# Premix on four quarters of TensorE's array, mix on its row halves, with five tokens to each piece

## The chip, the cores and the metric

The kernel runs on one core of a Trainium2 chip. The metric is the device time of one execution in microseconds (us). A core has a matrix engine (TensorE, PE in the profile, with its weight loads shown apart as PEld), a vector engine (VectorE, DVE), a scalar engine (ScalarE, ACT), a general engine (GpSimd, POOL) and a sync engine (SyncE, SP) that here issues nearly all DMAs. Sixteen DMA engines move data between the memory of the chip (HBM) and the core's on-chip memory (SBUF), and from one place of SBUF to another. Matmuls write to PSUM, an accumulator memory of its own.

## The reference

The kernel computes an attention that mixes its heads before and after the softmax, and behind it an MLP with `g = h - tanh(h)`:

```python
scale = 1.0 / np.sqrt(q.shape[-1])
scores = scale * np.matmul(q, k.transpose(0, 1, 3, 2))
scores = np.einsum('bhij,hg->bgij', scores, w_pre)
scores = scores - np.max(scores, axis=-1, keepdims=True)
attn = np.exp(scores)
attn = attn / (np.sum(attn, axis=-1, keepdims=True) + 1e-09)
attn = np.einsum('bhij,hg->bgij', attn, w_post)
attn_out = np.matmul(attn, v)
...
x = np.ascontiguousarray(attn_out.transpose(0, 2, 1, 3)).reshape(B * S, H * D)
h = x @ w_in
g = h - np.tanh(h)
return (g @ w_out).astype(np.float32)
```

q, k and v are (8, 12, 448, 64): B = 8 batches, H = 12 heads, S = 448 tokens, D = 64. `w_pre` and `w_post` are 12 x 12. x is 3584 x 768, `w_in` 768 x 2048, `w_out` 2048 x 768. All inputs and the output are float32.

## The kernel before

**Blocks, groups, places.** The 448 query tokens of a batch are cut in four blocks of 120, 120, 120 and 88, 32 blocks in all. The scores of a block lie in an SBUF tile `s` with tokens on partitions and [head, key] along each. To mix heads on TensorE, heads must lie on partitions, so a block is cut in groups of at most ten tokens, and a DMA, the gather (L493), brings a group from `s` into a tile `t` whose partitions are (token, head): 120 rows of 448 keys (108 for a group of nine). There are 360 groups. Two groups make one of 180 places, and a place is one turn of the loop that starts at L818. The MLP follows the loop.

**What a place does.** In written order, which every engine keeps: the copy out of PSUM of the mix before (`at`, L566 or L573); the gathers of groups 2p+4 and 2p+5; up to six other queued DMAs (`issue`, L370); `premix` of place p; `norm` of place p-1; `split` of group 2p+3; `expo` of place p; the jobs that the table `todo` has for the place; the scores' evictions from PSUM; `mix` of place p-1; and one step of the conversion of the MLP's weights (`conv`, helpers at L38 to L110, on ACT, DVE and GpSimd, with loads and stores of its own).

**Premix** (L508) multiplies a group with a block-diagonal matrix that holds `w_pre` ten times, `wpre` [120, 120]. The even group of a place takes one fp32 matmul (L512), which the hardware runs in two passes. The odd group is split beforehand: `th` is its value rounded to fp32r (L504, DVE), `tl` the rest (L505, GpSimd). It takes three fp32r matmuls of one pass each (L515 to L517), with `wpre` split likewise. The tiles `t` of even groups have three buffers, those of odd ones two.

**Expo, norm, mix.** `expo` takes the row maximum on DVE (L527) and the exponential on ACT (L529) with the row sum in `zs`. `norm` adds 1e-9 (L541), takes the reciprocal (L543), both on DVE, and makes one weight tile for each group on ACT: `wr = wpost / sum` (L545), with `wpost` the block-diagonal matrix of `w_post`. `mix` (L548) uses the exponentials `e` as weights of the array, 112 keys at a time, and moves `wr` through: eight fp32 matmuls of 120 columns (L557) into the one buffer of `ps_o`, which gives the mixed attention with keys on partitions.

**The jobs of `todo`.** Scores of two head pairs (L475): three fp32r matmuls for each head, the two heads of a pair on the two row halves of the array, since D = 64. Their evictions (L481) go to ACT and DVE for even pairs, both to ACT for odd ones. Values (L598): fp32 matmuls on the two column halves. Transposes of queries (L441) and keys (L415). Loads of queries, keys and values. A planner sets the places. The keys of a batch are loaded from one place before the place where block 1 of the batch before starts (L785), one of three tiles a place. Their transposes stand two places later or more (L791).

**DMA order.** SP issues its DMAs in written order, gathers and loads in one stream. A tile's buffers go round, so a gather can't be issued before the matmul (or the split) that read the tile's buffer last has ended.

The helper `halves` (L405) is `(slice(0, 64), slice(64, 128))`. NG = 360, NPL = 180, GI = 10, GP = 120.

Of the kernel before, what the change touches and what calls it, by code (L numbers as in the profile page):

```python
# [10 lines left out]
F32 = mybir.dt.float32  # L11
# [10 lines left out]
def raw(ap):  # L22

    return ap.bitcast(F32)
# [124 lines left out]
def kernel_body(  # L149
# [19 lines left out]
    GI = P // H  # L169
    MT = GI * H  # L170
    GP = GI * H
    starts = list(range(0, S, MT))
    sizes = [min(MT, S - s) for s in starts]
    NM = len(sizes)
# [162 lines left out]
    with ExitStack() as st:  # L337
# [127 lines left out]
        def scores(i, hp, engines=None):  # L465

            b, m = blocks[i]
            n = sizes[m]
            if hp == 0:
                sts[i] = sp.tile([MT, H, S], F32, name="s", tag="s")  # L470
            (qh, ql), (kh, kl) = qbs[i], kks[b, hp // 2]
            pss = [ps_m.tile([P, 512], F32, name="ps_q", tag="ps_m") for _ in halves]
            for x, (qx, kx) in enumerate(((qh, kh), (qh, kl), (ql, kh))):
                for a, ps in zip(halves, pss):
                    nc.tensor.matmul(ps[:n, :S], qx[a, hp, :], kx[a, hp % 2], start=(x == 0), stop=(x == 2))  # L475

            def rest():

                two = engines or (nc.scalar.copy, nc.scalar.copy if hp % 2 else nc.vector.tensor_copy)
                for j, (eng, ps) in enumerate(zip(two, pss)):  # L480
                    eng(sts[i][:n, 2 * hp + j, :], ps[:n, :S])  # L481

            sooner.append(rest)
# [7 lines left out]
        tg, ts, te = {}, {}, {}  # L491

        def gather(t, eng=nc.sync):  # L493
            i, g = groups[t]
            x = gp.tile([GP, S], F32, name="t", tag=f"t{t % 2}", bufs=3 - t % 2)
            eng.dma_start(x[: rows[t], :], sts[i][tokens[t].start : tokens[t].stop : tokens[t].step])
            tg[t] = x

        def split(t, eng=nc.gpsimd):
            n = rows[t]  # L500
            x = tg.pop(t)
            th = gp.tile([GP, S], F32R, name="th", tag="th", bufs=2)
            tl = gp.tile([GP, S], F32R, name="tl", tag="tl", bufs=2)
            nc.vector.tensor_copy(th[:n, :], x[:n, :])  # L504
            eng.tensor_sub(tl[:n, :], x[:n, :], raw(th[:n, :]))  # L505
            ts[t] = (th, tl)

        def premix(p):  # L508

            pa, pb = [ps_p.tile([P, S], F32, name="ps_p", tag="ps_p") for _ in range(2)]  # L510
            n = rows[2 * p]
            nc.tensor.matmul(pa[:n, :], wpre[:n, :n], tg.pop(2 * p)[:n, :], start=True, stop=True)  # L512
            n = rows[2 * p + 1]
            th, tl = ts.pop(2 * p + 1)
            nc.tensor.matmul(pb[:n, :], wph[:n, :n], th[:n, :], start=True, stop=False)  # L515
            nc.tensor.matmul(pb[:n, :], wpl[:n, :n], th[:n, :], start=False, stop=False)
            nc.tensor.matmul(pb[:n, :], wph[:n, :n], tl[:n, :], start=False, stop=True)  # L517
            return pa, pb

        def expo(p, pss):  # L520
            zs = gp.tile([GP, 3, 2], F32, name="zs", tag="zs")
            es = []
            for j, ps in enumerate(pss):
                n = rows[2 * p + j]

                mx = gp.tile([GP, 1], F32, name="mx", tag="mx")
                nc.vector.tensor_reduce(out=mx[:n, :], in_=ps[:n, :], axis=AX.X, op=ALU.max, negate=True)  # L527
                e = gp.tile([GP, S], F32, name="e", tag="e", bufs=4)
                nc.scalar.activation(  # L529
                    e[:n, :], ps[:n, :], AF.Exp, bias=mx[:n, :], scale=1.0, accum_out=zs[:n, 0, j : j + 1]  # L530
                )
                es.append(e)
            te[p] = [es, zs]

        def norm(p):
            zs = te[p][1]
            wr = gp.tile([GP, 2, P], F32, name="wr", tag="wr", bufs=2)[:, :, :GP]
            n0, n1 = rows[2 * p], rows[2 * p + 1]
            for j, n in enumerate((n0, n1)):

                nc.vector.tensor_scalar_add(zs[:n, 1, j : j + 1], zs[:n, 0, j : j + 1], 1e-9)  # L541
            for js, n in ((slice(0, 2), n0),) if n0 == n1 else ((slice(0, 1), n0), (slice(1, 2), n1)):
                nc.vector.reciprocal(zs[:n, 2, js], zs[:n, 1, js])  # L543
            for j, n in enumerate((n0, n1)):
                nc.scalar.mul(wr[:n, j, :], wpost[:n, :], zs[:n, 2, j : j + 1])  # L545
            te[p].append(wr)

        def mix(p):  # L548
            es, _, wr = te.pop(p)
            ps = ps_o.tile([P, 2, 512], F32, name="ps_o", tag="ps_o")  # L550
            for j, e in enumerate(es):
                i, g = groups[2 * p + j]
                n = rows[2 * p + j]
                if g == 0:
                    ats[i] = kp.tile([CP, NC, H, MT], F32, name="at", tag="at", bufs=2)
                for c in range(NC):
                    nc.tensor.matmul(  # L557
                        ps[:CP, j, c * GP : (c + 1) * GP], e[:n, c * CP : (c + 1) * CP], wr[:n, j, :],
                        start=True, stop=True,
                    )  # L560

            def rest():
                (i0, _), (i1, _) = groups[2 * p], groups[2 * p + 1]
# [84 lines left out]
        now()  # L648
        load_q(2)
        now()  # L650
        tmp_w = kp.tile([P, 2 * GP + 2 * H], F32, name="tmp_w", tag="at", bufs=2)
        w12 = tmp_w[:H, 2 * GP : 2 * GP + 2 * H].rearrange("p (w h) -> p w h", w=2)
        nc.scalar.dma_start(w12[:, 0, :], w_pre)
        nc.scalar.dma_start(w12[:, 1, :], w_post)

# [8 lines left out]
        def scores_of(i, hq):  # L664
# [7 lines left out]
        prep_q(0, 1)  # L672
        flush()

        repeat = tmp_w[:H, GP : 2 * GP]
        nc.gpsimd.memset(repeat, 0.0)
        nc.gpsimd.affine_select(
            out=repeat.rearrange("p (i h) -> p i h", i=GI), in_=repeat.rearrange("p (i h) -> p i h", i=GI),
            compare_op=ALU.not_equal, fill=1.0, base=0, pattern=[[0, GI], [-1, H]], channel_multiplier=1,
        )  # L680
        ps_w = bank()[:GP, : 2 * H].rearrange("p (w g) -> p w g", w=2)
        nc.tensor.matmul(ps_w.rearrange("p w g -> p (w g)"), repeat, w12.rearrange("p w g -> p (w g)"), start=True, stop=True)
        wpre, wpost = [cst.tile([GP, P], F32, name=x)[:, :GP] for x in ("wpre", "wpost")]
        pre_v = wpre.rearrange("p (i g) -> p i g", i=GI)
        post_v = wpost.rearrange("p (g i) -> p g i", i=GI)
        nc.vector.tensor_copy(pre_v, ps_w[:, 0, :].unsqueeze(1).to_broadcast([GP, GI, H]))
        nc.vector.tensor_copy(post_v, ps_w[:, 1, :].unsqueeze(2).to_broadcast([GP, H, GI]))
        for x, step in ((pre_v, [[H, GI], [0, H]]), (post_v, [[0, H], [H, GI]])):

            nc.gpsimd.affine_select(  # L690
                out=x, in_=x, compare_op=ALU.is_ge, fill=0.0, base=0, pattern=[[-a, n] for a, n in step],
                channel_multiplier=1,
            )
            nc.gpsimd.affine_select(
                out=x, in_=x, compare_op=ALU.is_ge, fill=0.0, base=H - 1, pattern=step, channel_multiplier=-1,
            )


        busy(3, ps_b)
# [17 lines left out]
        prep_q(1, 0)  # L717
        prep_q(1, 1)
        flush()
        wph, wpl = [cst.tile([GP, P], F32R, name=x)[:, :GP] for x in ("wph", "wpl")]  # L720
        nc.vector.tensor_copy(wph, wpre)
        nc.vector.tensor_sub(wpl, wpre, raw(wph))
# [6 lines left out]
        split(1, nc.vector)  # L729
# [88 lines left out]
        for p in range(NPL + 3):  # L818
# [117 lines left out]
```

## Time and profile before

| what | value |
| --- | --- |
| runs, median (all) | 1879.54 us (1880.68, 1879.54, 1875.44) |
| profiled execution | 1880.95 us |
| its span | 1879.2 us |
| its granted TensorE clock | 0.998 |
| ACT's exponentials L529, in 360 instructions | all on 120 or 108 partitions |
| HBM traffic over the span | 156 GB/s |

The span is the profiled time from the first to the last instruction. The page cuts it in 40 slices of 47 us and gives the busy share of each engine in tenths; the MLP begins in slice 20:

```profile
## 2 busy tenths in 40 slices
PE   8999999999999999999999999999999999999998
...
DVE  5676766767776676766456556556566566565555
ACT  5787887878888788788634443434434434433433
POOL 2344444444444345444201000000000000000000
...
DMA packets 232795, 371.92 MB, mean 198 GB/s; under 512 B 98992, under 2 KB 207536, under 8 KB 218288
```

A digit of 9 is 90% or more. In the loop (the left half) PE is busy throughout, ACT to 70 or 80%, DVE to 60 or 70%, GpSimd to 40%; DMA is the mean share of the sixteen DMA engines, so 6 can be all of them at 60% or ten of them at nearly all.

### The profile page before, as it was taken

The page shows a single profiled execution, that of the slowest core. Times are in us where ns is not written, and L with a number is a line of the kernel's source. Part 1 is how long each engine was busy: PE and PEld are TensorE (multiplying, and loading weights), DVE is VectorE, ACT ScalarE, POOL GpSimd, SP SyncE. Part 2 cuts the span into 40 slices and gives each one's busy share as a digit, 9 for nine tenths or more (in the row PEclk, how much of TensorE's full clock was granted, in tenths as well). Part 3 has the DMA queues.
Part 4 walks back from the last instruction along what each step waited for, and adds up shares of the span by engine and source line. Part 5 has one row for each costly group of instructions (what it writes and reads, how often), then busy time and mean ns, then how long its engine had stood idle before and what let it go on. Part 6 is the DMA issues. An engine that isn't in the chain of part 4 may idle for free.

```text
span 1879.2 us, 35344 instructions
## 1 busy us (share of the span) xinstructions
PE 1851.1 (99%) x13150; PEld 1525.9 (81%) x13150; DVE 1184.7 (63%) x2457; ACT 1133.8 (60%) x2503; POOL 451.9 (24%) x401
## 2 busy tenths in 40 slices
PE   8999999999999999999999999999999999999998
PEld 6777887787878777877788888888888888888887
DVE  5676766767776676766456556556566566565555
ACT  5787887878888788788634443434434434433433
POOL 2344444444444345444201000000000000000000
PEclk9999999999999999999999999999999999999999
DMA  6667658676675757656565565665655655655651
GB/s 162 183 183 201 189 166 221 182 208 190 177 216 171 209 177 205 195 164 189 212 255 193 206 246 192 223 218 196 235 213 196 235 205 196 237 209 191 233 193 42
DMA packets 232795, 371.92 MB, mean 198 GB/s; under 512 B 98992, under 2 KB 207536, under 8 KB 218288
## 3 DMA queue, kind: packets, MB, share of 16 engines
q1 hardware_dynamic: 231740, 368.45, 60.5%
q8 instruction: 104, 1.70, 0.4%
q10 hardware_dynamic: 884, 1.22, 0.2%
q14 instruction: 67, 0.55, 0.1%
HBM read 245.37 MB, written 47.19 MB: 156 GB/s over the span
## 4 chain that ended last, share of the span: by engine, by line
PE 86%; DMA 6%; ACT 3%; DVE 2%; issue 2%; POOL 1%; SPq 0%; ACTq 0%; POOLq 0%; DVEq 0%
PE ps_o L557 13%; PE ps_h L256 8%; PE ps_h L260 8%; PE ps_h L255 8%; PE ps_m L598 7%; PE ps_p L512 6%; PE ps_q L475 6%; PE ya L303 5%; PE ya L300 5%; PE ya L301 5%; DMA t<-s 4%; PE yb L303 3%; PE yb L301 3%; PE yb L300 3%; PE ps_p L517 2%
## 5 line engine op out<-in xcount | busy, mean ns | idle before, releaser
L557 PEld LDWEIGHTS ps_o<-wr,e 120*112 120x112 f32 (+1 forms) x2880 | 307.2, 177 | 49.8 <-issue 30.1
L557 PE MATMUL ps_o<-wr,e 120*112 120x120 f32 (+1 forms) x2880 | 340.5, 271 | 4.1 <-ACT wr L545 4.1
L527 DVE TENSOR_REDUCE mx<-ps_p 120x1 f32<-120x448 f32 x360 | 218.6, 622 | 136.9 <-PE ps_p L512 136.7
L505 POOL TENSOR_TENSOR tl<-t,th 120x448 fp32r<-120x448 f32 x179 | 204.4, 1142 | 391.8 <-DVE th L504 221.5
L287 ACT CAST gh<-r 128x512 fp32r<-128x512 f32 x112 | 69.6, 621 | 373.3 <-DVE r L280 373.3
L256 PE MATMUL ps_h<-xl,w 128*128 128x512 f32 x672 | 263.2, 392 | 0.5 <-POOL pad L222 0.5
L255 PE MATMUL ps_h<-xh,w 128*128 128x512 f32 x672 | 262.8, 391 | 0.0
L529 ACT ACTIVATE e<-ps_p,mx 120x448 f32<-120x448 f32 x360 | 225.8, 636 | 36.7 <-DVE mx L527 36.1
L245 POOL TENSOR_TENSOR xl<-rx,xh 128x512 fp32r<-128x512 f32 x38 | 53.7, 1415 | 741.3 <-ACT xh L244 741.3
L566 ACT COPY at<-ps_o 112x960 f32<-112x960 f32 x156 | 154.5, 990 | 113.4 <-PE ps_o L557 112.5
L303 PE MATMUL ya<-w,gl 128*128 128x512 f32 x448 | 177.1, 395 | 0.7 <-DVE gl L288 0.7
L276 DVE SCALAR_TENSOR_TENSOR r<-qa,ps_h 128x512 f32<-128x512 f32 x112 | 77.0, 687 | 158.7 <-ACT t L273 158.7
L300 PE MATMUL ya<-w,gh 128*128 128x512 f32 x448 | 175.0, 391 | 1.3 <-ACT gh L287 1.3
L301 PE MATMUL ya<-w,gh 128*128 128x512 f32 x448 | 174.9, 390 | 0.0
L260 PE MATMUL ps_h<-xh,w 128*128 128x512 f32 x672 | 170.5, 389 | 0.0
L512 PE MATMUL ps_p<-t,wpre 120*120 120x448 f32 x360 | 165.7, 542 | 4.3 <-ACT e L529 3.5
L598 PE MATMUL ps_m<-at,vr 112*64 112x120 f32 (+1 forms) x3072 | 163.3, 263 | 1.9 <-ACT at L566 1.5
L598 PEld LDWEIGHTS ps_m<-at,vr 112*64 112x64 f32 x3072 | 149.7, 138 | 14.7 <-ACT at L566 3.7
L270 ACT ACTIVATE u<-ps_h 128x512 f32<-128x512 f32 x112 | 66.9, 597 | 149.2 <-PE ps_h L260 149.2
L260 PEld LDWEIGHTS ps_h<-xh,w 128*128 128x128 f32 x672 | 126.1, 188 | 26.2
L256 PEld LDWEIGHTS ps_h<-xl,w 128*128 128x128 f32 x672 | 126.6, 188 | 24.6 <-POOL pad L222 0.9
L255 PEld LDWEIGHTS ps_h<-xh,w 128*128 128x128 f32 x672 | 126.6, 188 | 22.9
(102 smaller groups left out, 3622.0 us busy)
## 6 DMA issues: line engine op xcount, KB each, us to landing
w<-ws SPq DMA_DIRECT2D x112, 1536.0 KB
t<-s SPq DMA_DIRECT2D x342, 210.0 KB
cr<-in_moe_w_in_dram SPq DMA_DIRECT2D x24, 512.0 KB
cr<-in_moe_w_out_dram SPq DMA_DIRECT2D x32, 384.0 KB
vr<-in_v_dram SPq DMA_DIRECT2D x24, 448.0 KB
kr<-in_k_dram SPq DMA_DIRECT2D x23, 448.0 KB
out_dram<-ob SPq DMA_DIRECT2D x24, 384.0 KB
qr<-in_q_dram SPq DMA_DIRECT2D x23, 360.0 KB
```

The costliest lines, as they stand in the source:

```text
L255: nc.tensor.matmul(ph, wh[:, fs], xh, start=(c == 0), stop=False)
L256: nc.tensor.matmul(ph, wh[:, fs], xl, start=False, stop=False)
L260: nc.tensor.matmul(ph, wl[:, fs], xh, start=False, stop=(c == NK - 1))
L300: nc.tensor.matmul(y, gh[:, tok], wh[:, es], start=first, stop=False)
L301: nc.tensor.matmul(y, gh[:, tok], wl[:, es], start=False, stop=False)
L303: nc.tensor.matmul(y, gl[:, tok], wh[:, es], start=False, stop=last)
L505: eng.tensor_sub(tl[:n, :], x[:n, :], raw(th[:n, :]))
L512: nc.tensor.matmul(pa[:n, :], wpre[:n, :n], tg.pop(2 * p)[:n, :], start=True, stop=True)
L527: nc.vector.tensor_reduce(out=mx[:n, :], in_=ps[:n, :], axis=AX.X, op=ALU.max, negate=True)
L529: nc.scalar.activation(e[:n, :], ps[:n, :], AF.Exp, bias=mx[:n, :], scale=1.0, accum_out=zs[:n, 0, j : j + 1])
L557: nc.tensor.matmul(ps[:CP, j, c * GP : (c + 1) * GP], e[:n, c * CP : (c + 1) * CP], wr[:n, j, :], start=True, stop=True,)
L598: nc.tensor.matmul(pv[j * D : (j + 1) * D, r, :n], vt[:, j, c, :], ats[i][:, c, 2 * hp + j, :n], start=(c == 0), stop=(c == NC - 1),)
```

## The change

**Gather.** A group is gathered in two halves, one DMA each. Tokens 0 to 4 go to partitions 0 to 59 of a `t` tile that now has 128 partitions, tokens 5 to 9 to partitions 64 to 123. A group of nine has halves of five and four. Tile tags and buffer counts stay as they were.

**Premix.** `split` and its tiles go. A place's premix is four fp32 matmuls of at most 60 x 64 on the four quarters of the array: row half `a` holds the tokens of half r, column half `to` sets the partitions of the output. Group j of the place comes out on partition half j, and PSUM tile r holds half r of both groups. `wpre` is 128 x 64, the block-diagonal matrix of five tokens on both partition halves, with columns 60 to 63 zero.

**Expo, norm, mix.** `expo` works on 128 partitions. `norm` has two adds, one reciprocal, and one product on GpSimd (L538) for the 128 x 2 x 60 weights of the place, in place of two on ACT. `mix` has 16 matmuls of 60 moving columns and at most 60 weight rows: group j on row half j, with the output columns of half r written with a stride.

**Evictions and keys.** Scores' evictions always go to one ACT and one DVE copy. The keys' loads start three places earlier (four before the block's start), and their transposes stand four places later than the load or more, not two. **Set-up.** The block-diagonal matrices are built in two halves each, with eight selects on GpSimd, four copies and two adds on DVE.

Order on SP, in the first places of the loop (a tile's name with its number, `s` the block's scores, `kr` a tile of keys). Before:

```order
L496 DMA t_645<-s_317 120x1x448
L496 DMA t_647<-s_317 120x1x448
L367 DMA kr_634<-in_k_dram 112x16x64
L496 DMA t_716<-s_317 120x1x448
L496 DMA t_718<-s_317 120x1x448
L367 DMA kr_691<-in_k_dram 112x16x64
L496 DMA t_803<-s_317 120x1x448
L496 DMA t_805<-s_317 120x1x448
```

After:

```order
L505 DMA t_457<-s_216 60x1x448 x2
L505 DMA t_460<-s_216 60x1x448 x2
L505 DMA t_502<-s_216 60x1x448 x2
L505 DMA t_505<-s_216 60x1x448 x2
L369 DMA kr_483<-in_k_dram 112x16x64
L505 DMA t_562<-s_330 60x1x448 x2
L505 DMA t_565<-s_330 60x1x448 x2
L369 DMA kr_537<-in_k_dram 112x16x64
```

Each gather has become two issues; other loads keep their place in the stream among them.

Order on PE, in the middle of the loop: one place with scores, and the next with values. Before:

```order
L512 MATMUL ps_p<-t,wpre 120x448
L515 MATMUL ps_p<-th,wph 120x448
L516 MATMUL ps_p<-th,wpl 120x448
L517 MATMUL ps_p<-tl,wph 120x448
L475 MATMUL ps_q<-kk,qh 120x448 x4
L475 MATMUL ps_q<-kk,ql 120x448 x2
L475 MATMUL ps_q<-kk,qh 120x448 x4
L475 MATMUL ps_q<-kk,ql 120x448 x2
L557 MATMUL ps_o<-wr,e 112x120 x8
```

After:

```order
L516 MATMUL ps_p<-t,wpre 64x448 x4
L477 MATMUL ps_q<-kk,qh 120x448 x4
L477 MATMUL ps_q<-kk,ql 120x448 x2
L477 MATMUL ps_q<-kk,qh 120x448 x4
L477 MATMUL ps_q<-kk,ql 120x448 x2
L555 MATMUL ps_o<-wr,e 112x12x5 x16
L516 MATMUL ps_p<-t,wpre 64x448 x4
L597 MATMUL ps_m<-at,vr 64x120 x24
L555 MATMUL ps_o<-wr,e 112x12x5 x16
```

The order of the stages is the same. Premix has one form of four matmuls instead of four of two kinds, and mix has twice as many of half the width.

Order on GpSimd, in the middle of the loop (`cm`, `cl`: conversion of the MLP's weights). Before:

```order
L505 TENSOR_TENSOR tl<-t,th 120x448
L104 TENSOR_TENSOR cl<-cm,cs 128x512
L505 TENSOR_TENSOR tl<-t,th 120x448
L96 TENSOR_TENSOR cm<-cr,cs 128x384
L98 TENSOR_TENSOR cm<-cm,cr 128x384
```

After:

```order
L538 TENSOR_TENSOR wr<-wpost,zs 128x2x60
L96 TENSOR_TENSOR cm<-cr,cs 128x512
L538 TENSOR_TENSOR wr<-wpost,zs 128x2x60
L98 TENSOR_TENSOR cm<-cm,cr 128x512
L538 TENSOR_TENSOR wr<-wpost,zs 128x2x60
```

Where the split's second half stood, once a place, the product that the mix of the same place reads now stands.

```diff
-                two = engines or (nc.scalar.copy, nc.scalar.copy if hp % 2 else nc.vector.tensor_copy)
+                two = engines or (nc.scalar.copy, nc.vector.tensor_copy)
...
         def gather(t, eng=nc.sync):
             i, g = groups[t]
-            x = gp.tile([GP, S], F32, name="t", tag=f"t{t % 2}", bufs=3 - t % 2)
-            eng.dma_start(x[: rows[t], :], sts[i][tokens[t].start : tokens[t].stop : tokens[t].step])
+            x = gp.tile([P, S], F32, name="t", tag=f"t{t % 2}", bufs=3 - t % 2)
+            tok, n = tokens[t], half_rows(t)
+            src = lambda u: sts[i][u[0] : u[-1] + 1 : u.step]
+            for a, u in zip(halves, (tok[:GH], tok[GH:])):
+                eng.dma_start(x[a.start : a.start + H * len(u), :], src(u))
             tg[t] = x
...
         def premix(p):
...
+            pss = [ps_p.tile([P, S], F32, name="ps_p", tag="ps_p") for _ in halves]
+            ts = [tg.pop(2 * p + j) for j in range(2)]
+            for j, to in enumerate(halves):
+                for r, (a, ps) in enumerate(zip(halves, pss)):
+                    k = slice(a.start, a.start + H * half_rows(2 * p + j)[r])
+                    nc.tensor.matmul(ps[to, :], wpre[k, :], ts[j][k, :], start=True, stop=True)
+            return pss
...
         def norm(p):
...
-            for j, n in enumerate((n0, n1)):
-                nc.scalar.mul(wr[:n, j, :], wpost[:n, :], zs[:n, 2, j : j + 1])
+            nc.vector.reciprocal(zs[:, 2], zs[:, 1])
+            nc.gpsimd.tensor_mul(
+                wr, wpost[:, :HP].unsqueeze(1).to_broadcast([P, 2, HP]), zs[:, 2].unsqueeze(2).to_broadcast([P, 2, HP])
+            )
...
         def mix(p):
...
-                    nc.tensor.matmul(
-                        ps[:CP, j, c * GP : (c + 1) * GP], e[:n, c * CP : (c + 1) * CP], wr[:n, j, :],
-                        start=True, stop=True,
-                    )
+                    for j, a in enumerate(halves):
+                        k = slice(a.start, a.start + H * half_rows(2 * p + j)[r])
+                        nc.tensor.matmul(
+                            ps[:CP, j, c * GP : (c + 1) * GP].rearrange("p (h i) -> p h i", i=GI)[:, :, r * GH : (r + 1) * GH],
+                            e[k, c * CP : (c + 1) * CP], wr[k, r, :],
+                            start=True, stop=True,
+                        )
...
-            p, o, done = first[blocks.index((b - 1, 1))] // 2 - 1, 0, []
+            p, o, done = first[blocks.index((b - 1, 1))] // 2 - 4, 0, []
...
-                o = max(p + 2, o + 1)
+                o = max(p + 4, o + 1)
...
-            if p + 1 < NPL:
-                split(2 * p + 3)
```

The line numbers of the code after are those of the changed program; its helper `half_rows(t)` gives the tokens of a group's two halves, GH = 5 and HP = 60.

More of the change, by code (lines that the diff above doesn't have):

```diff
@@ L499, in split @@
[L499 to L506, printed above, removed]
-        def premix(p):
[L510 to L518, printed above, removed]
+            x = gp.tile([P, S], F32, name="t", tag=f"t{t % 2}", bufs=3 - t % 2)
@@ L520, in expo @@
         def expo(p, pss):
-            zs = gp.tile([GP, 3, 2], F32, name="zs", tag="zs")
+            zs = gp.tile([P, 3, 2], F32, name="zs", tag="zs")
             es = []
[L523 to L530, printed above, removed]
-                )
+            for r, ps in enumerate(pss):
+                mx = gp.tile([P, 1], F32, name="mx", tag="mx")
+                nc.vector.tensor_reduce(out=mx, in_=ps, axis=AX.X, op=ALU.max, negate=True)
+                e = gp.tile([P, S], F32, name="e", tag="e", bufs=4)
+                nc.scalar.activation(e, ps, AF.Exp, bias=mx, scale=1.0, accum_out=zs[:, 0, r : r + 1])
@@ L683, in kernel_body @@
[L683 to L696, printed above, removed]
+        for a in halves:
+            nc.gpsimd.affine_select(
+                out=repeat[:, a][:, :HP].rearrange("p (i h) -> p i h", i=GH),
+                in_=repeat[:, a][:, :HP].rearrange("p (i h) -> p i h", i=GH),
+                compare_op=ALU.not_equal, fill=1.0, base=0, pattern=[[0, GH], [-1, H]], channel_multiplier=1,
+            )
@@ new lines, in kernel_body @@
+        ps_w = bank()[:, : 2 * H].rearrange("p (w g) -> p w g", w=2)
+        nc.tensor.matmul(ps_w.rearrange("p w g -> p (w g)"), repeat, w12.rearrange("p w g -> p (w g)"), start=True, stop=True)
+        wpre, wpost = [cst.tile([P, D], F32, name=x) for x in ("wpre", "wpost")]
+        both = tmp_w[:, P : P + 2 * 2 * HP].rearrange("p (w a n) -> p w a n", w=2, a=2)
+        for w in range(2):
+            for a in range(2):
+                if w == 0:
+                    x = both[:, w, a].rearrange("p (i g) -> p i g", i=GH)
+                    of, step = ps_w[:, w, :].unsqueeze(1).to_broadcast([P, GH, H]), [[H, GH], [0, H]]
+                else:
+                    x = both[:, w, a].rearrange("p (g i) -> p g i", i=GH)
+                    of, step = ps_w[:, w, :].unsqueeze(2).to_broadcast([P, H, GH]), [[0, H], [H, GH]]
+                nc.vector.tensor_copy(x, of)
+                nc.gpsimd.affine_select(
+                    out=x, in_=x, compare_op=ALU.is_ge, fill=0.0, base=-D * a, pattern=[[-m, n] for m, n in step],
+                    channel_multiplier=1,
+                )
+                nc.gpsimd.affine_select(
+                    out=x, in_=x, compare_op=ALU.is_ge, fill=0.0, base=D * a + H - 1, pattern=step,
+                    channel_multiplier=-1,
+                )
@@ L699, in kernel_body @@
+        for w, x in enumerate((wpre, wpost)):
+            nc.gpsimd.memset(x[:, HP:], 0.0)
+            nc.vector.tensor_add(x[:, :HP], both[:, w, 0], both[:, w, 1])
         busy(3, ps_b)
```

36 lines of the change are left out of this document (14 added, 22 removed).

## The prediction

> **What bounds the kernel now.** I read the page first, then three stretches of the span, then one place of the loop in the chain and on the engines, and last the DMA side of the gathers, which the change doubles in number.
>
> ```profile
> PE 1851.1 (99%) x13150; PEld 1525.9 (81%) x13150; DVE 1184.7 (63%) x2457; ACT 1133.8 (60%) x2503; POOL 451.9 (24%) x401
> PE 86%; DMA 6%; ACT 3%; DVE 2%; issue 2%; POOL 1%; SPq 0%; ACTq 0%; POOLq 0%; DVEq 0%
> ```
> TensorE holds 86% of the chain that ended last. The windows below (columns: stretch, length, busy time of each engine, granted clock, DMA share, GB/s) give the loop of 180 places, from the first premix at 24.10 to the last at 930.91, and four short stretches used further down.
>
> ```profile
> 24.10:930.91 906.81, 890.98 (x8171) 713.26 (x8172) 624.40 (x1635) 733.80 (x1819) 395.45 (x349) 1.00 0.64 189
> 22.70:26.10 3.40, 2.39 (x10) 0.92 (x6) 2.25 (x5) 0.97 (x2) 0.00 (x0) 1.00 0.66 247
> 133.70:134.50 0.80, 0.80 (x9) 0.49 (x6) 0.80 (x2) 0.80 (x3) 0.00 (x0) 1.00 0.65 251
> 234.85:235.55 0.70, 0.70 (x10) 0.70 (x9) 0.24 (x2) 0.70 (x3) 0.00 (x0) 1.00 0.58 225
> ```
> The change touches only the loop and its set-up: 906.8 us, 5.04 a place. The 948 us behind it are the MLP and stay. Inside a place the chain in order of time reads, for a place with scores and the next one with values:
>
> ```profile
> 502.20 0.75 PE ps_p L512 x2
> 502.95 0.20 PE ps_p L515
> 503.15 0.21 PE ps_p L516
> 503.36 0.20 PE ps_p L517
> 503.56 1.43 PE ps_q L475 x11
> 504.98 1.82 PE ps_o L557 x16
> 506.81 0.75 PE ps_p L512 x2
> ...
> 508.17 1.97 PE ps_m L598 x48
> 510.14 1.82 PE ps_o L557 x16
> ```
> Nothing but TensorE stands there, so TensorE sets 4.61 us (502.20 to 506.81), of which premix has 1.36 and mix 1.82. The DMA share of 0.64 looks like slack. It is a mean over 16 engines, and the next part is about what it hides.
>
> **TensorE's part: a gain.** Premix before is one fp32 matmul of two passes (0.75 together, 0.375 each) and three fp32r ones of 0.20. After, it is four fp32 matmuls of two passes on four quarters of the array. Whether quarters run at once is not in this trace, but halves are:
>
> ```profile
> 508.10 0.30 PE L598 MATMUL ps_m<-at,vr 112*64 112x88 f32 x2
> 508.10 0.20 PEld L598 LDWEIGHTS ps_m<-at,vr 112*64 112x64 f32 x4 [0.31 <-ACT at L566]
> 503.49 0.28 PEld L475 LDWEIGHTS ps_q<-kk,qh 64*120 64x120 f32 x4 [0.31 <-ACT at L566]
> 503.80 0.18 PEld L475 LDWEIGHTS ps_q<-kk,ql 64*120 64x120 f32 x2
> 504.91 0.17 PEld L557 LDWEIGHTS ps_o<-wr,e 120*112 120x112 f32 x1 [0.32 <-issue]
> 504.91 0.27 PEld L557 LDWEIGHTS ps_o<-wr,e 120*112 120x112 f32 x2 [0.32 <-issue]
> ```
> Two matmuls of values on two column halves fill one 0.30, and four score loads on two row halves end 0.28 after the first began, where a pair takes 0.18: two rounds of 0.10. So halves work side by side, rows and columns alike, and I take all four quarters to: 0.75 plus 0.02 of issue, 0.59 less than 1.36. The other end is two at a time, 1.5, a loss of 0.14.
>
> Mix after is 16 matmuls of 60 moving columns in place of 8 of 120. The streaming halves, the weights do not: they are still 112 columns per pass. The last two rows show the price: one load ends after 0.17, two after 0.27, so a load of 112 columns holds its path 0.10 (0.095 by 0.10 a load for 120 columns). 16 rounds, both row halves at once, come to 16 x 0.095 = 1.52. Of the 1.82 now, 0.18 is the change of array form ahead of it (16 x 0.1025 = 1.64 is the rest). Scores and mix now use the same row halves, so that 0.18 goes in places with scores, and 0.16 comes ahead of premix, whose form is new. A place with scores: 0.77 + 0.16 + 1.43 + 1.52 = 3.88, that is 0.73 less. One with values: 0.77 + 0.16 + 1.97 + 0.18 + 1.52 = 4.60 against 5.15, 0.55 less. By the program's order 92 places hold scores, 22 values alone, 40 values or the like with transposes (a further change of form, 0.38 less), 25 neither (bound by the run from copy to mix, I take 0.2 less): 67 + 12 + 15 + 5 = **99 us** that TensorE could give back.
>
> **ACT, DVE and GpSimd: hidden.** Rows of these groups (busy, mean ns of one):
>
> ```profile
> L545 ACT ACTIVATE wr<-wpost,zs 120x120 f32<-120x120 f32 x344 | 118.7, 399 | 3.0 <-DVE zs L543 2.8
> L504 DVE CAST th<-t 120x448 fp32r<-120x448 f32 x172 | 77.9, 453 | 50.2 <-DMA t<-s 50.2
> L481 ACT COPY s<-ps_q 120x448 f32<-120x448 f32 x212 | 99.1, 547 | 6.5 <-PE ps_q L475 6.2
> L481 DVE COPY s<-ps_q 120x448 f32<-120x448 f32 x76 | 47.2, 622 | 14.0 <-PE ps_q L475 13.9
> L505 POOL TENSOR_TENSOR tl<-t,th 120x448 fp32r<-120x448 f32 x171 | 195.3, 1142 | 380.4 <-DVE th L504 219.2 <-issue 59.1 <-PE ps_o L557 45.0
> ```
> ACT loses L545 (125 us) and 96 copies of 0.55 (53); DVE loses L504 (82) and gains those 96 at 0.62 (60): from 734 and 624 us busy in the loop to about 556 and 602, under any place time here. GpSimd loses 204 of L505 and gains 180 products of 128x120. No row has that form; L505 scaled by columns gives 1142 x 120/448 = 0.31, a whole L505 is the upper end, I take 0.4. It waits in GpSimd's queue behind up to two converting steps, and mix(p-1) waits for it: 0 to 0.5 in places with scores, some 10 us in all if TensorE is the bound, and nothing if something else is.
>
> The earlier loads of keys are aimed at waits like this one, ahead of which the load was issued one place late:
>
> ```profile
> 57.53 1.73 PE L415 MATMUL ps_m<-ident,kr 112*128 112x112 f32 x8 [3.26 <-ACT e L529]
> ```
> Worth 0 to 10 us; I take 6 where TensorE is the bound, 0 where it is not.
>
> **The gathers: a loss, and the larger term.** A gather brings 10 tokens x 12 heads x 448 x 4 bytes = 215 KB, its source ten partitions of s. In the stretch 22.70 to 26.10 four of them, issued within 1.2 us on two queues,
>
> ```profile
> 21.07 5.60 SPq L496 DMA_DIRECT2D t<-s  x4
> 21.28 1.81 ACTq L496 DMA_DIRECT2D t<-s  x2
> ```
> run and nothing else does: 247 GB/s, 860 KB in 3.48 us, 0.87 each, at a share of 0.66. Alone, at 133.70, one has 251 GB/s and the same 0.65. So four queued gathers go no faster than one: each fills ten of the sixteen engines (10/16 = 0.63), one per token, and always the same ten. The row at 234.85 is a gather of nine tokens: 0.58 and 225 GB/s, nine tenths of 251, as nine engines would (9/16 = 0.56). An engine moves 25 GB/s.
>
> The change cuts each gather into two of five tokens. One engine per token puts a half on five engines, for the same 12 rows each: 107.5 KB at 125 GB/s, **0.86 us a half**; if the set is fixed, the halves follow each other on the same five. The other ends: the halves lie on ten different engines (0.86 a pair, no loss), or are dealt over all sixteen (a gain of three eighths).
>
> The Trainium skill, in "DMA: Bandwidth & Descriptors", section "Why a DMA increments its semaphore by 16 and not by 1", says that a DMA issued from SP or ACT runs on the largest number of engines up to 16 that divides the slowest dimension of both its patterns, and on the lowest-numbered ones. By that rule a half with 5 source partitions and 60 rows gets five, the lowest, each time, and the sum below stays as it is; ten and nine agree with it, five is in no run here.
>
> The sum for those five engines: 720 halves x 0.86 = 619 us. The rest of the traffic: 0.64 x 906.8 = 580 us on every engine, less the gathers' present part, 360 x 0.87 x 0.66 = 207, leaves 373, which other loads and stores spread over all sixteen (keys, queries, values, converted weights). 619 + 373 = **992 us** of work that must fit in a loop of 907, where the ten busiest engines have 360 x 0.87 + 373 = 686 now. So DMA becomes the bound, at 5.5 us a place, above TensorE's 4.5. What they idle comes on top: bounds 0 and 180 x 1.57 = 283 (issue at 21.07 to the first packets at about 22.65, once a place). The gathers are issued two to three places ahead, so the queue rarely runs dry; I take 30, for the start and for the last sixteen places, which convert nothing. Loop 1022. TensorE's 99 us then turn into waits ahead of premix, and the terms above cost or bring nothing.
>
> SP's own issue is close behind:
>
> ```profile
> L496 SPq DMA_DIRECT2D t<-s x294: 768/790/5422, 152.5 to 895.2; - x147
> ```
> Nine-token gathers take SP as long as ten-token ones (minimum 768), so I take 0.79 for a half: four make 3.2 us a place plus about 1.3 for the other issues, 4.5. That is under 5.5, but as long as TensorE's place.
>
> **Sum.** The profiled execution took 1880.95 (span 1879.2), 1.4 over the median 1879.54. 1880.95 - 906.8 + 1022 = **1996**.
>
> **The rivals.**
> *Halves do not share engines* (the other side: faster). Mechanism: the two halves of a gather go to different engines; the place is the DMA queue; it decides as soon as a half has eight or more engines or its own five, since then the busiest have 686 us or less of work. Price: none, and TensorE stays the bound: 1880.95 - 99 + 10 - 6 = **1786**, up to 1830 if SP's 4.5 us a place binds. For it: no row shows a five-token DMA. Against it: ten and nine tokens went by tokens, and queued gathers never spread onto the six idle engines. Chance 0.16.
> *Quarters take turns* in that world: the second pass of a quarter must wait for its first, and if no later quarter may start before it, four quarters of two passes last 5 x 0.375 = 1.88 instead of 0.77, 1.11 x 180 = 200 us: **1986**. Against it: the two value matmuls that begin at 508.10 together have two passes each. Chance 0.04. The Trainium skill has this rule in "TensorE: Matmul & The Clock Gate", "Part 3: Packing small matmuls — row/col tiling": matmuls start and end strictly in order. The trace does not bear it out for two tiles with two passes each.
> *Five engines, better packed*: the other traffic overlaps on an engine, its 373 shrinks by a fifth, loop 918 to 990, **1890 to 1950**; part of the forecast's chance below.
>
> **How the numbers follow.** Five engines 0.80 (of which 0.04 end within 0.3% of the time before or just under it), different engines 0.16, turns 0.04. Likeliest, on its own: 1940 to 2090, the low end with the packing just named, the high end with 100 us more idling. To leave out no more than 0.2 the range must go from 1860 to 2110; the faster case lies outside. Runs of this kernel spread by 0.28%, so 0.3% is what can be told from no change. Faster 0.17, same 0.03, slower 0.80.
>
> **What would show it.** If right: in the loop the gather-only stretches have a DMA share near 0.33 and 125 GB/s; premix waits for t<-s in most places, 1 to 2 us; a place lasts about 5.6; TensorE's busy share in the loop falls under 85%; premix itself takes 0.77 and mix about 1.5. If wrong: a share of 0.6 or more in those stretches, no premix waiting for DMA, and the chain all TensorE at about 3.9 in a place with scores. A half-gather issued in under 0.5 us would take SP out; a product of over 1 us on GpSimd would put it in.

## The result, and the profile after

The changed kernel takes 1949.1 us (median of 4 runs, 1947.44 to 1956.13), the kernel before 1877.49 (1875.19 to 1880.68). The ratio is 1.0387, 95% interval 1.0356 to 1.0419: slower by 72 us. The profiled execution took 1948.63, its span is 1946.5.

From the page after (busy time of the engines, the granted clock by slices of 49 us, the chain that ended last):

```profile
PE 1871.0 (96%) x16570; PEld 1480.3 (76%) x16570; DVE 1136.2 (58%) x2362; ACT 1006.2 (52%) x2051; POOL 315.5 (16%) x409
PEclk9899998999989899799989999999999999999999
PE 79%; DMA 10%; SPq 3%; ACT 3%; DVE 2%; issue 1%; POOL 1%; ACTq 0%; POOLq 0%; DVEq 0%
```

TensorE has 79% of the chain, 86% before; DMA has 10% for 6%, and SP, which had none, 3%. The clock shows dips in the loop. The windows of the trace after (columns: stretch, length, busy time of each engine, granted clock, DMA share, GB/s) are the loop, two stretches in which little but gathers runs, and the start of the MLP; the last row is the start of the MLP in the kernel before.

```profile
24.96:989.33 964.37, 905.42 (x11557) 662.54 (x11557) 574.81 (x1534) 607.63 (x1372) 255.83 (x348) 0.93 0.59 177
25.00:38.00 13.00, 11.15 (x87) 6.04 (x88) 5.72 (x15) 6.43 (x15) 0.77 (x2) 0.74 0.33 122
356.80:365.20 8.40, 8.40 (x136) 7.17 (x134) 5.24 (x14) 4.72 (x13) 3.36 (x5) 1.00 0.33 126
989.33:1000.00 10.67, 5.61 (x58) 4.68 (x56) 3.49 (x11) 5.34 (x11) 0.77 (x2) 0.64 0.92 318
```

```profile
930.91:942.00 11.09, 9.25 (x55) 6.99 (x54) 3.62 (x9) 7.83 (x17) 2.73 (x3) 1.00 0.67 273
```

The loop went from 906.8 to 964.4 us, 57.6 more; what lies behind it from 948.3 (1879.2 - 930.91) to 957.2 (1946.5 - 989.33), 8.9 more. The stretch behind the loop shows where: TensorE is busy for 5.61 of 10.67 us at a clock of 0.64, while DMA is at 0.92. In the chain there, the loads of the MLP's first tile (`rx`) follow the landing of the last gather, at 986.72, and end at 991.85, after the start of the last premix at 989.33.

In the gather stretches the DMA share is 0.33 and the rate 122 to 126 GB/s, half of the 0.65 and 247 to 251 of before. That is what five engines would give for a half of five tokens, if two halves share them; the experiments below ask whether it is that.

Where the loop lost it, the chain of waits shows in order of time:

```profile
485.27 0.91 PE ps_p L516 x8
486.19 1.42 PE ps_q L477 x12
487.61 1.53 PE ps_o L555 x32
489.14 0.91 PE ps_p L516 x8
```

```profile
494.78 0.49 SPq L369
495.27 0.05 issue
495.32 6.74 DMA cr<-in_moe_w_in_dram
...
502.15 0.43 DVE cm L80
502.58 0.14 DVE zs L536 x2
...
503.08 0.39 POOL wr L538
503.47 0.04 issue
503.51 2.62 PE ps_o L555 x31
```

The first four rows are a place with scores: 3.87 us (485.27 to 489.14) in place of 4.61, all TensorE. The others are a stall: a load of MLP weights, issued behind gathers, lands 6.74 us later; the converting step that needs it stands on DVE ahead of the adds of `norm`, so these, GpSimd's product and mix all wait for it. The mix that comes out of the stall lasts 2.62 in place of 1.53, at half clock. TensorE's own waits in the changed kernel (us in total, times, longest):

```profile
PE ps_o L555 <- POOL wr L538: 21.1, 19, 3.9
PE ps_m L597 <- DMA vr<-in_v_dram: 16.0, 7, 3.4
PE ps_p L516 <- DMA t<-s: 8.9, 16, 1.5
PEld ps_p L516 <- DMA t<-s: 49.9, 70, 2.3
```

The waits of premix for its gather (70 of weight loads and 16 of matmuls) fall in about 50 of the 180 places; in other places the load that is late is another.

### The profile page after: what moved, and what is told of

Same layout as the page of the kernel before. It is cut to its first block, busy times and chain, and to the rows that moved or that the text cites. A ratio compares the mean times of both kernels' runs of the same rounds, so it can differ in the third digit from the quotient of the medians.

```text
span 1946.5 us, 41891 instructions
## 1 busy us (share of the span) xinstructions
PE 1871.0 (96%) x16570; PEld 1480.3 (76%) x16570; DVE 1136.2 (58%) x2362; ACT 1006.2 (52%) x2051; POOL 315.5 (16%) x409
## 4 chain that ended last, share of the span: by engine, by line
PE 79%; DMA 10%; SPq 3%; ACT 3%; DVE 2%; issue 1%; POOL 1%; ACTq 0%; POOLq 0%; DVEq 0%
PE ps_o L555 11%; PE ps_p L516 8%; PE ps_h L257 8%; PE ps_h L258 8%; PE ps_h L262 8%; PE ps_m L597 7%; PE ya L305 5%; PE ya L302 5%; PE ya L303 5%; PE ps_q L477 5%; DMA t<-s 4%; PE yb L305 3%; PE yb L303 3%; PE yb L302 3%; SPq L505 3%; DMA cr<-in_moe_w_in_dram 2%
## 5 line engine op out<-in xcount | busy, mean ns | idle before, releaser
L555 PEld LDWEIGHTS ps_o<-wr,e 60*112 60x112 f32 (+1 forms) x5760 | 321.4, 183 | 60.0 <-POOL wr L538 38.9
L555 PE MATMUL ps_o<-wr,e 60*112 60x60 f32 (+1 forms) x5760 | 330.5, 267 | 27.4 <-POOL wr L538 21.1
L525 DVE TENSOR_REDUCE mx<-ps_p 128x1 f32<-128x448 f32 x360 | 209.9, 618 | 202.5 <-PE ps_p L516 201.5
L527 ACT ACTIVATE e<-ps_p,mx 128x448 f32<-128x448 f32 x360 | 225.6, 632 | 182.3 <-DVE mx L525 179.5
L516 PE MATMUL ps_p<-t,wpre 60*64 60x448 f32 (+1 forms) x1440 | 257.9, 594 | 11.6 <-DMA t<-s 8.9
L597 PE MATMUL ps_m<-at,vr 112*64 112x120 f32 (+1 forms) x3072 | 176.8, 275 | 25.5 <-DMA vr<-in_v_dram 16.0
L597 PEld LDWEIGHTS ps_m<-at,vr 112*64 112x64 f32 x3072 | 161.2, 146 | 50.4 <-DMA vr<-in_v_dram 13.2
L538 POOL TENSOR_TENSOR wr<-wpost,zs 128x120 f32<-128x120 f32 x180 | 69.9, 389 | 537.6 <-DVE zs L537 410.7
```

The source lines that it names most:

```text
L516: nc.tensor.matmul(ps[to, :], wpre[k, :], ts[j][k, :], start=True, stop=True)
L525: nc.vector.tensor_reduce(out=mx, in_=ps, axis=AX.X, op=ALU.max, negate=True)
L527: nc.scalar.activation(e, ps, AF.Exp, bias=mx, scale=1.0, accum_out=zs[:, 0, r : r + 1])
L555: nc.tensor.matmul(ps[:CP, j, c * GP : (c + 1) * GP].rearrange("p (h i) -> p h i", i=GI)[:, :, r * GH : (r + 1) * GH], e[k, c * CP : (c + ...
L597: nc.tensor.matmul(pv[j * D : (j + 1) * D, r, :n], vt[:, j, c, :], ats[i][:, c, 2 * hp + j, :n], start=(c == 0), stop=(c == NC - 1),)
```

## The experiments

The theory: halves of five tokens run on five DMA engines, always the same, and bound the loop. Rivals: SP's two issues for each gather; the two buffers of odd groups, which nothing frees early now that the split is gone; the new order of work on DVE and GpSimd. All ratios are to the kernel before.

**The halves alone, in the kernel before.** `old_tokens` cuts its gather by tokens:

```diff
-            eng.dma_start(x[: rows[t], :], sts[i][tokens[t].start : tokens[t].stop : tokens[t].step])
+            for a, u in ((0, tokens[t][: GI // 2]), (GI // 2 * H, tokens[t][GI // 2 :])):
+                eng.dma_start(x[a : a + H * len(u), :], sts[i][u[0] : u[-1] + 1 : u.step])
```

> The kernel before, with nothing changed but its gathers, cut in two DMAs of five tokens each to the same 120 partitions. Theory (engines): the five lowest engines have 720 x 0.86 = 619 us of gathers and some 350 of the rest, loop 950 to 990 in place of 907, total 1920 to 1965. Rival 1 (SP): 4.5 us of issues a place against 5.04 of TensorE, 1875 to 1890. Rival 2: as rival 1, no change.

Measured: 1961.39, ratio 1.0445 (1.0423 to 1.0467). `old_keys` cuts it by keys, two halves of 224 keys for all ten tokens:

```diff
-            eng.dma_start(x[: rows[t], :], sts[i][tokens[t].start : tokens[t].stop : tokens[t].step])
+            for ks in (slice(0, S // 2), slice(S // 2, S)):
+                eng.dma_start(x[: rows[t], ks], sts[i][tokens[t].start : tokens[t].stop : tokens[t].step, :, ks])
```

> The kernel before, with its gathers cut in two DMAs by keys, ten tokens and 224 keys each, 896 bytes a piece in place of 1792. Theory (engines): the same ten engines, the same bytes, 1870 to 1890; above that only if pieces of half the size cost more than half the time. Rival 1 (SP): the same range, since SP's 4.5 us stay under 5.04; a rise here as large as by tokens would speak for SP.

Measured: 1898.72, ratio 1.0108 (1.0086 to 1.0129). As many DMAs and as many bytes; by keys they cost 21 us, by tokens 84. So some 63 us hang on which dimension is cut, which in the theory sets the count of engines. The other 21, 9 more than the upper end of what was expected, hang on the doubled issues or the smaller pieces; these two were not taken apart. The total wait of `split` for gathers, which was 50.2 us in the kernel before, shows the same, first for `old_tokens`, then for `old_keys`:

```profile
DVE th L505 <- DMA t<-s: 221.5, 113, 6.9
DVE th L505 <- DMA t<-s: 59.3, 34, 7.2
```

The start of the loop shows the engines. Until about 25 us SP and ACT both issue gathers, and these run in the first stretch below, so that there one engine's issues do not set the pace; later SP issues alone. That stretch of `old_tokens`, then the same and the next one of `old_keys`:

```profile
25.00:28.00 3.00, 1.03 (x3) 0.64 (x3) 0.74 (x2) 0.97 (x2) 0.00 (x0) 0.82 0.33 124
```

```profile
25.00:28.00 3.00, 2.87 (x11) 1.58 (x13) 1.65 (x4) 0.97 (x2) 0.15 (x1) 0.87 0.64 218
28.00:32.00 4.00, 4.00 (x19) 2.31 (x17) 2.98 (x9) 3.48 (x10) 2.15 (x2) 0.67 0.38 131
```

In the first stretch halves by tokens get 124 GB/s at a share of 0.33, halves by keys 218 at 0.64: five engines and ten. In the second, halves by keys come at only 131 GB/s, little more than those by tokens in the first: SP starts one about every 0.85 us there, and an estimate from this pace is 107.5 KB / 0.85 us = 126 GB/s. So the 122 to 126 GB/s of the changed kernel's later gather stretches could not, by themselves, tell five engines from SP's issues.

**One gather in the changed kernel, in fixed buffers.** The ten tokens go to partitions 4 to 123 in one DMA, with four zero rows and a shifted `wpre` below. `one_keys` is the same with two DMAs by keys.

```diff
-            x = gp.tile([P, S], F32, name="t", tag=f"t{t % 2}", bufs=3 - t % 2)
...
-            for a, u in zip(halves, (tok[:GH], tok[GH:])):
-                eng.dma_start(x[a.start : a.start + H * len(u), :], src(u))
+            x = tts[t % 2][t // 2 % (3 - t % 2)]
+            eng.dma_start(x[PAD : PAD + rows[t], :], sts[i][tokens[t].start : tokens[t].stop : tokens[t].step])
...
-                    k = slice(a.start, a.start + H * half_rows(2 * p + j)[r])
+                    k = slice(a.start, a.start + (H * half_rows(2 * p + j)[r] if r else D))
```

> The changed kernel, but a group's ten tokens come in one DMA again, to partitions 4 to 123, so that the lower row half holds rows 4 to 63 (rows 0 to 3 zero, wpre shifted by four) and the upper one rows 64 to 123. Theory (a half of five tokens runs on five DMA engines, always the same, and these bound the loop): the gathers spread over ten engines again, 360 x 0.87 = 313 us on each beside some 370 of other traffic, well under TensorE; the 153 us by which places exceed the median of their kind and the 9 us at the MLP's start go, 1780 to 1810. Rival 1 (SP's issues bound the loop): the same, as 360 issues of 0.75 go too. Rival 2 (the waits come from the new order: the weights' product behind GpSimd's converting steps, the adds of norm behind DVE's): they stay, 1900 or more.

> As the run before it, but each gather is cut in two DMAs by keys: ten tokens and 224 keys each, so ten engines and half the bytes each, and as many issues by SP as in the changed kernel. Theory (engines): 1780 to 1830, the upper end if SP's 4.5 us a place touches TensorE's 4.5. Rival 1 (SP's issues): 1920 to 1950, as in the changed kernel.

Measured: 2063.09 and 2122.44. These two say nothing on the theory. With tiles of fixed buffers, two for odd groups, the gather of group 2p+5 stood ahead of the premix of place p in the same buffer, so that odd groups were mixed from later tokens and each premix waited for a gather issued in its own place:

```profile
PEld ps_p L517 <- DMA t<-s: 212.1, 100, 5.9
PE ps_p L517 <- DMA t<-s: 136.9, 83, 5.1
```

They led to the buffers as a rival of their own.

**Gathers and buffers, apart.** `one_two` writes the odd gather, and the place's other queued DMAs with it, behind the premix that frees its buffer; `one_three` gives odd groups three buffers and has both gathers ahead of premix again; `halves_three` is the changed kernel with three buffers; `keys_three` is `one_three` with each gather cut by keys. The edit of `halves_three`, which is all that it changes:

```diff
-            x = gp.tile([P, S], F32, name="t", tag=f"t{t % 2}", bufs=3 - t % 2)
+            x = gp.tile([P, S], F32, name="t", tag=f"t{t % 2}", bufs=3)
```

> The changed kernel with one DMA of ten tokens for each group, to partitions 4 to 123, and the odd group's gather written behind the premix that frees its buffer (two buffers for odd groups, as in the changed kernel; in the first try it stood ahead of it). Engines theory (a half of five tokens uses five DMA engines, which bound the loop): 1785 to 1830. Rival (odd gathers come late because two buffers no longer suffice without the split that freed them early): 1900 or more, with premix waiting for odd gathers.

> As the run before it, with three buffers for odd groups and both gathers at the start of a place. Engines theory: 1780 to 1810, at most 20 below the run before it. Rival (buffers): 1780 to 1810 here, but 100 less than the run before it.

> The changed kernel as it is, halves of five tokens in two DMAs, with three buffers for odd groups. Engines theory: five engines keep their 619 us of gathers beside the other traffic, 1925 to 1955. Rival (buffers): 1790 to 1840.

> As one_three, with each gather cut by keys into two DMAs of ten tokens and 224 keys: ten engines, and SP's four issues a place as in the changed kernel. Engines theory: within 40 us above one_three (cutting by keys cost the kernel before 21). Rival (SP's issues bound the changed kernel): 1900 to 1950.

| run | DMAs per gather | engines of each | odd buffers | us | ratio (95%) |
| --- | --- | --- | --- | --- | --- |
| changed kernel | 2 | 5 | 2 | 1949.1 | 1.0387 (1.0356 to 1.0419) |
| halves_three | 2 | 5 | 3 | 1929.1 | 1.0270 (1.0253 to 1.0287) |
| keys_three | 2 | 10 | 3 | 1823.0 | 0.9712 (0.9685 to 0.9740) |
| one_two | 1 | 10 | 2 | 1831.0 | 0.9750 (0.9735 to 0.9764) |
| one_three | 1 | 10 | 3 | 1788.0 | 0.9523 (0.9507 to 0.9539) |

From the changed kernel down to `one_three`, in this order: the third buffer 20 us, ten engines for five 106, one issue for two (or whole pieces for halves) 35. The engines are the largest part by far. Two of the steps change more than their name says: from `halves_three` to `keys_three` the tiles also become fixed buffers with four zero rows and the pieces halve, and `one_two` also issues its other loads later than `one_three`. For the engines alone the clean pair is `old_tokens` and `old_keys`. Taken back from the fast version, the single DMA costs 35 us, and the third buffer 43 with those later loads. The windows over the loops of `halves_three`, `keys_three` and `one_three`:

```profile
25.00:977.60 952.60, 898.53 (x11556) 660.26 (x11556) 575.09 (x1534) 607.09 (x1373) 256.64 (x348) 0.93 0.60 180
```

```profile
25.86:866.52 840.66, 804.58 (x11557) 619.80 (x11557) 565.95 (x1534) 600.95 (x1372) 257.36 (x348) 0.98 0.69 203
```

```profile
25.10:834.86 809.76, 786.34 (x11556) 608.40 (x11557) 567.38 (x1538) 600.14 (x1371) 257.21 (x348) 1.00 0.72 212
```

The loop of `one_three` is 97 us shorter than before, at full clock. This version beats both kernels, by 90 and by 161 us. It has the changed kernel's order of work on DVE and GpSimd, so that order is not what makes the changed kernel slow.

**The smaller edits, one by one on `one_three`.** `lead_old` puts the keys' loads back, `wr_act` the two ACT instructions for mix's weights, `evict_old` the old evictions:

```diff
-            p, o, done = first[blocks.index((b - 1, 1))] // 2 - 4, 0, []
+            p, o, done = first[blocks.index((b - 1, 1))] // 2 - 1, 0, []
...
-                o = max(p + 4, o + 1)
+                o = max(p + 2, o + 1)
```

```diff
-            nc.gpsimd.tensor_mul(
-                wr, wpost[:, :HP].unsqueeze(1).to_broadcast([P, 2, HP]), zs[:, 2].unsqueeze(2).to_broadcast([P, 2, HP])
-            )
+            for r in range(2):
+                nc.scalar.mul(wr[:, r, :], wpost[:, :HP], zs[:, 2, r : r + 1])
```

```diff
-                two = engines or (nc.scalar.copy, nc.vector.tensor_copy)
+                two = engines or (nc.scalar.copy, nc.scalar.copy if hp % 2 else nc.vector.tensor_copy)
```

> one_three (the changed kernel with one DMA of ten tokens a group and three buffers for odd groups; 1788) with the keys' loads where they were before, one place ahead of the block in place of four, transposes two places later or more in place of four. The prediction's step (the earlier loads are worth 0 to 10, taken as 6, where TensorE is the bound): 1788 to 1798. Rival (with shorter places the lead of two is no longer enough): 1805 or more, waits of the transposes for keys.

Measured: 1821.38, ratio 0.9689 (0.9673 to 0.9705), 33 us above `one_three`. The rival holds; TensorE's longest wait there is one that `one_three` does not have:

```profile
PE ps_m L417 <- DMA kr<-in_k_dram: 22.7, 6, 5.8
```

> one_three with the weights of mix made by two ACT instructions a place again, now 128x60 each, and none on GpSimd. The prediction's step (the product waits in GpSimd's queue, some 10 us of the loop, and ACT's time is hidden): 1775 to 1788. Rival (ACT, which also makes the exponentials and the copies, becomes what mix waits for): 1795 or more.

Measured: 1797.33, ratio 0.9553 (0.9532 to 0.9574). The interval overlaps that of `one_three`, so the 9 us are not certain; that GpSimd's product costs 10 us more than ACT's two is not borne out.

> one_three with the scores' evictions of odd pairs both on ACT again. The prediction's step (hidden, either way): 1783 to 1793. Rival (ACT's second copy in a row holds up the next place's scores or exponentials, now that a place with scores lasts 3.86): 1800 or more.

Measured: 1802.68, ratio 0.9595 (0.9571 to 0.9620): 15 us above, between the two expectations.

`mix_old` is `wr_act` with mix as it was, and so with ACT products of 128x120 in place of 128x60; it does not put the tokens back in order within their block. The part of the edit in mix:

```diff
-                    for j, a in enumerate(halves):
...
+                    nc.tensor.matmul(
+                        ps[:CP, r, c * GP : (c + 1) * GP], e[:, c * CP : (c + 1) * CP], wr[:, r, :],
+                        start=True, stop=True,
+                    )
```

> wr_act with mix as before: eight matmuls of 120 columns over the full 128 rows a place, with ACT's two products of 128x120. The tokens of a place come out in another order within their block, since the columns are not put back. The prediction's step (mix 1.52 against 1.64, and a change of array form of 0.18 ahead of it in places with scores): 92 x 0.3 + 88 x 0.12 = 38 above wr_act, 20 to 50. Rival (the row halves bring nothing, because the weight loads set the pace in both): within 10 of wr_act.

Measured: 1803.73, ratio 0.9593 (0.9580 to 0.9607), only 6 above `wr_act`. The chain says that the rival is wrong all the same. A place with scores in `mix_old`, then parts of two in `one_three`:

```profile
507.37 0.91 PE ps_p L517 x8
508.28 1.37 PE ps_q L477 x12
509.66 1.82 PE ps_o L553 x16
```

```profile
500.76 1.53 PE ps_o L556 x32
502.29 0.91 PE ps_p L517 x8
...
509.21 1.40 PE ps_q L477 x12
```

Mix lasts 1.82 against 1.53, 0.29 more. The gain is there on TensorE, and much of it turns into waits and a lower clock. The loops of `mix_old` and of `wr_act`:

```profile
23.77:854.87 831.10, 814.43 (x8709) 608.14 (x8709) 562.76 (x1538) 699.68 (x1727) 191.18 (x170) 1.00 0.70 206
```

```profile
25.22:848.41 823.19, 798.26 (x11556) 616.11 (x11557) 566.58 (x1538) 681.58 (x1727) 190.75 (x170) 0.98 0.72 208
```

TensorE is busy for 16.2 us less in the second, but sits idle for 24.9 in place of 16.7 (831.10 - 814.43), and its clock is 0.98: about 2 x 0.02 x 823 = 33 us at half rate, an estimate that takes the clock as either 1 or 0.5, as in the stretches of the last section.

## Why the prediction was right, point by point

**TensorE's 99 us: right.** `one_three` shows them once nothing covers them: the loop is 906.8 - 809.8 = 97 us shorter, TensorE is busy for 104.6 less (890.98 to 786.34) and idle for 7.6 more. That the waits stay so small takes the third buffer, the earlier keys and the new evictions as well. A place with scores went from 4.61 to 3.87 (forecast 3.88), premix with the change of form to 0.91 (0.93), mix to 1.53 (1.52). The rival in which quarters take turns falls with the 0.91; it needed 1.88 for premix alone.

**Five engines a half: right.** While two queues issue, halves of five tokens get the share and rate of five engines and halves by keys those of ten, and cutting by keys in place of tokens is worth 63 us in the kernel before. The rule of the Trainium skill ("DMA: Bandwidth & Descriptors", "Why a DMA increments its semaphore by 16 and not by 1") gave five for this shape, and the trace agrees: 0.33 x 16 = 5.3.

**The loop of 1022: right in kind, 58 us too long, and the term that was mis-sized is the other traffic's 373.** It was taken from the mean DMA share, as if a share of 1 were a full engine set. It is not: in the kernel before

```profile
168.00:172.00 4.00, 4.00 (x30) 3.15 (x31) 3.96 (x11) 3.88 (x11) 1.87 (x2) 1.00 1.23 199
```

the share is 1.23 at 199 GB/s, so the times of packets on one engine overlap, and a share counts some of the work twice. The loop of 964.4 leaves at most 964 - 619 = 345 for the rest of the work on the five engines. Reckoned by shares, as the prediction did it, the changed kernel itself would have 0.59 x 964 - 720 x 0.86 x 0.33 = 364 beside the 619, and 983 us do not fit in 964. How the 58 us divide between this and the 30 of idle time was not measured. The case of better packing, which had a loop of up to 990, is the one that came. That the time lies inside the range is luck in part: the overstated 373 makes the sum too long, and the slow clock (last section) and the buffers, which the sum does not have, work the other way.

**The shape of the wait: wrong.** I had premix wait 1 to 2 us in most places, a place last about 5.6 us, and TensorE's busy share under 85%. In places of the common kind TensorE keeps its own pace of 3.87; where a load of values or weights stands among the gathers, as in the stall above, the wait is long and stands elsewhere: at a converting step on DVE, at mix, at values. The profile says 94% busy (905 of 964), part of it at half clock.

**SP's issues: not settled for the changed kernel.** A half takes SP 0.745 (median of the changed kernel's gathers), where 0.79 was taken:

```profile
L505 SPq DMA_DIRECT2D t<-s x716: 667/745/5292, 22.0 to 981.3; - x179
```

As many issues, on ten engines, give 1823 (`keys_three`), near the 1830 that the faster rival had if SP's 4.5 us a place binds. What SP's issues add where five engines already bound the loop was not tried.

**The buffers: not in the prediction.** The split read an odd group a place early and freed its buffer. Without it two buffers cost 20 us in the changed kernel, 43 in the fast one, there with the later loads of `one_two`. I counted split's time and missed what it did for the next transfer.

**ACT, DVE and GpSimd hidden: nearly.** The product on GpSimd takes 0.389 (0.4 was taken), and it costs no more than ACT's two. ACT's busy time in the loop is 607.6 where about 556 were forecast, DVE's 574.8 where 602 were; neither is the bound. The evictions are worth 15 us where they were to be worth none. The earlier keys are worth 33 where TensorE is the bound, not 6: the price was read from one wait of 3.26 in a loop with places of 4.6, and shorter places make the same lead shorter.

**What lies behind the loop stays: 8.9 us off,** since loads of the MLP's first tiles queue behind the last gathers.

So the faster rival, at 1786, sized the changed TensorE work rightly; `one_three` is that kernel without the five engines, at 1788. It also has the third buffer, which the rival did not count on and which is worth up to 43, so that only 2 us lie between them is luck in part.

## What to carry to other kernels

Before cutting a DMA, ask which dimension is cut: here ten tokens on the slowest one gave ten engines, five gave five, and the same halves cut by keys kept ten. A low mean share of DMA engines can be a few engines at their limit; look at a stretch in which one kind of transfer runs alone, and in which its issues do not set the pace. And a step that is dropped may have freed a buffer early: follow the buffer, not only the time.

## What the runs showed that was not expected

TensorE's clock can fall after short waits. In the changed kernel, around the stall shown above:

```profile
503.51 1.32 PE L555 MATMUL ps_o<-wr,e 60*112 60x60 f32 x18 [2.45 <-POOL wr L538]
```

```profile
494.00:503.50 9.50, 5.72 (x52) 3.26 (x52) 3.65 (x11) 3.10 (x7) 0.43 (x2) 1.00 0.74 191
503.50:508.00 4.50, 4.49 (x41) 2.98 (x42) 2.65 (x8) 4.15 (x9) 2.33 (x3) 0.58 0.64 196
508.00:510.50 2.50, 2.50 (x20) 2.19 (x21) 1.54 (x4) 1.84 (x6) 0.00 (x0) 0.50 0.33 124
514.50:518.30 3.80, 3.80 (x56) 2.88 (x56) 2.81 (x5) 3.08 (x7) 0.00 (x0) 1.00 0.24 89
```

The clock is still 1.00 through the wait of 2.45 us, falls to 0.5 at about 504.2, when TensorE works again, and stays there until about 511. Over the loop 0.93 is granted, so about 2 x 0.07 x 964 = 135 us run at half rate, against almost none before. The Trainium skill ("TensorE: Matmul & The Clock Gate", "Part 1: The HAM clock gate") has the clock halved after an idle window of some 3.4 us; here no wait in the 9.5 us before the fall was longer than 2.45. The loop is 154.6 us longer than that of `one_three`; TensorE is idle for 35.5 us more of it and busy for 119.1 more, and half of the 135, some 68, is the most that the slow clock can have added to the busy time. How much of the loss is the waits themselves and how much the slow clock behind them was not taken apart: while the DMA engines are the bound, a slow TensorE also gives them time to catch up.
